# Two row tiles of TensorE: another order of seven products, another giver for one semaphore

## The chip, the cores and the metric

The kernel runs on one NeuronCore of a Trainium2 chip. The metric is the device time of one execution in microseconds (us), median of several runs. Engines are named as in the profile: PE is TensorE's matmul, PEld its weight load, DVE is VectorE, ACT is ScalarE, POOL is GpSimd, SP issues the DMAs.

## The reference

Sigmoid attention over 8 batches, 12 heads, 448 tokens and head width 64, and after it a gated feed-forward layer over the 3584 tokens (768 to 1536 to 768):

```python
scores = scale * np.matmul(q, k.transpose(0, 1, 3, 2)) - np.log(S)
attn = 1.0 / (1.0 + np.exp(-scores))
x = np.matmul(attn, v)                       # (8, 12, 448, 64) -> (3584, 768)
...
gate = 1.0 / (1.0 + np.exp(-(x @ w_gate)))
val = x @ w_val
y = gate * val @ w_out
```

All inputs are float32 (the three weights arrive as 64-bit words, which DVE turns into float32 on the chip).

## The kernel before

**Two stages.** Attention takes the first 257 us; in it, scores and values are matmuls of 64x64 tiles (lines 208 and 224). After a g-th block of scores, `LAG` = 2 blocks later, comes the same block of values. PSUM then holds two score buffers of two banks (`sc`) and four one-bank sums of values (tags `av00`, `av01`, `av10`, `av11`). The rest, the feed-forward layer, is the helper at line 341: 9072 matmuls of 64 rows by 128 columns by 448 tokens.

**Seven products.** Each matrix product of the layer is cut into 2x2 blocks and done with seven block products instead of eight (Strassen's scheme in Winograd's form). x and the weights come as seven sums of blocks each; product i multiplies the i-th of both. Products are summed in PSUM as far as they can be: 1 is added onto 0, 3 and 4 onto 2, 6 onto 5. So an accumulator begins at 0, 2 and 5 and is read after *every* product, since each partial sum is wanted: product 0 gives `s1`, 1 the block "11", 2 `u2`, 3 `u3`, 4 a new `s1`, 5 a new `u3`, 6 a new `u2`. A product that adds onto an accumulator may start only when the sum before it has been read out of the bank (evacuated) by DVE (line 391) or ACT (lines 515 and 522).

**Input stage** (to about 880 us): three passes `s` over the hidden blocks, in each four pairs of batches `p`, in each seven products `i`, in each four accumulators `q` (gate and value of two hidden blocks). A *unit* is one accumulator of one product: 3 blocks of 128 rows x 3 terms. The terms are there because float32 operands are split into a high and a low part in a faster format, and three of the four products of parts are summed. ACT makes the high part (line 169 for x, 417 for weights), DVE the low part (172, 420).

**Output stage** (from about 880 us): four pairs, seven products, in each two halves of the hidden blocks, in each three accumulators `o`. Half 1 adds onto half 0 without evacuation between.

**Two row tiles.** The 128 rows of TensorE are used as two tiles of 64 rows that work at the same time. Of every unit, nine matmuls go to the upper tile (lane 0: partitions 0 to 63 of weights and x) and nine to the lower tile (lane 1: partitions 64 to 127), onto the *same* accumulator. They must not meet in that bank, so the lower nine come later: `BEHIND` = 12 matmuls behind. `Lanes.push` writes the instruction stream: one upper matmul of the unit at hand, one lower matmul of an earlier unit, in turn. So the lower lane begins a unit just after the upper lane has issued the fourth matmul of the unit that follows.

**Semaphores between the lanes.** `mark` lets a matmul raise a lane's semaphore when it is done (the drain is fused into the matmul issued last), and notes for an accumulator which count means that its matmuls are done. `follow` waits for that count. Before, the mark of an upper half hangs on the *second matmul of the next* upper unit (`n == 1`, line 372), that of a lower half on the second matmul of the next lower unit (line 358). The first lower matmul of a unit waits for lane 0's mark, the first upper matmul of a product that adds onto an accumulator waits for lane 1's mark and for the engine that evacuated the bank.

**What sets the order of the rest.** DVE, ACT and POOL get their work unit by unit, in the order in which lower halves are finished: `after_in` (input stage) and `after_out` (output stage) issue the evacuation of the unit, then the preparation of the x operand two products ahead, now and then the low part of a weight tile (`low_w`), and steps of the weight conversion (lines 116 to 134) at an even rate. Each engine works its list in order. DMAs stand in SP's queue.

Of the kernel before, what the change touches and what calls it, by code (L numbers as in the profile page):

```python
# [17 lines left out]
P = 128  # L18
# [10 lines left out]

NP = 7  # L30


@with_exitstack
def sigmoid_attention_glu_kernel(ctx: ExitStack, tc: tile.TileContext, qk, v, wg, wv, wo, out):
# [123 lines left out]

    x_order = [(s, p, i) for s in range(NPASS) for p in range(NPAIR) for i in range(NP)]
    x_loaded, ops = {}, {}  # L160
# [24 lines left out]
    with tc.manual_schedule(), tc.tile_pool(name="att", bufs=2) as att, tc.tile_pool(name="sc", bufs=2, space=PSUM) as scp, \  # L185
# [9 lines left out]
        def load_v(m):  # L195
            if m < B * NQ:
                loads[m].append(att.tile([P, 7, 2, D], F32, tag="v", name="v"))
                if m > 0:
                    nc.sync.dma_start(out=loads[m][1], in_=v[m // NQ, m % NQ])

        def scores(m, g):
            qkt = loads[m][0]
            sc = scp.tile([P, 2, 512], F32, tag="sc", name="sc")
            for h in range(2):
                for u in range(2):
                    p = u if g == 3 else g // 4
                    k0 = S + (3 * P if g == 3 else g % 4 * P + u * HP)
                    nc.tensor.matmul(sc[halves[u], h, :S], lhsT=qkt[halves[h], p, k0:k0 + HP], rhs=qkt[halves[h], p, :S],  # L208
                                     start=True, stop=True)
            a = att.tile([P, 2, S], F32, tag="a", name="a", bufs=3)  # L210
            nc.scalar.activation(a, sc[:, :, :S], AF.Sigmoid, bias=bias, scale=scale)  # L211
            return a

        def values(m, g, a):
            vt = loads[m][1]
            for u in range(2):
                p = u if g == 3 else g // 4
                key = (2 * m + p, u)
                start = key not in avs
                if start:  # L220
                    avs[key] = avp.tile([P, 512], F32, tag=f"av{p}{u}", name="av")
                last = (3 if u == 0 else 2) if p == 0 else 6
                for h in range(2):
                    nc.tensor.matmul(avs[key][halves[h], :S], lhsT=vt[halves[u], g, h], rhs=a[halves[u], h],  # L224
                                     start=start, stop=g == last)
            if g == 3:
                finish(2 * m)
            if g == 6:
                finish(2 * m + 1)
# [85 lines left out]
    with tc.manual_schedule(), tc.tile_pool(name="mm", bufs=8, space=PSUM, reuse_waits="tile") as mm:  # L315
# [14 lines left out]
        class Lanes:  # L330


            def __init__(self):
                self.behind, self.skip, self.at, self.ended = [], BEHIND, 0, {}
                self.sems, self.count = [tc.alloc_semaphore(f"lane{h}") for h in range(2)], [0, 0]
                self.last = [None, None]

# [15 lines left out]
            def lower(self):  # L353
                unit, key, done = self.behind[0]
                if self.at == 0:
                    self.follow(key)
                ins = self.one(1, unit, self.at)
                if self.at == 1 and self.last[1] is not None:
                    self.mark(self.last[1], 1)
                self.at += 1  # L360
                if self.at == len(unit[1]):
                    self.last[1] = key
                    self.at = 0
# [3 lines left out]
            def push(self, unit, key, done):  # L367
                self.behind.append((unit, key, done))
                self.follow(key)
                for n in range(len(unit[1])):  # L370
                    ins = self.one(0, unit, n)
                    if n == 1 and self.last[0] is not None:
                        self.mark(self.last[0], 0)
                    if self.skip:
                        self.skip -= 1
                    else:
                        self.lower()
                self.last[0] = key

            def drain(self):  # L380
                self.mark(self.last[0], 0)
                while self.behind:
                    self.lower()
# [12 lines left out]
        nextW = {}  # L396
        o_order = [(p, i, h) for p in range(NPAIR) for i in range(NP) for h in range(2)]
        h_loaded, h_ops, wx = {}, {}, {}
# [28 lines left out]
        def fetch_wx(i):  # L427
            tag, bufs = (("wr", 3), ("wf", 2), ("wsum", 2))[0 if i < 3 else 1 if i < 5 else 2]
            wx[i] = block(tag, bufs, [P, HJ - NQUAD, 2, HW], F32R)
# [48 lines left out]
        def outputs():  # L478
            m = 0
            for p in range(NPAIR):  # L480
                st = [{} for _ in range(HC)]
                for i in range(NP):
                    if p == 0:
                        W[i] = nextW[i]
                    for half in range(2):
                        for o in range(HC):
                            d = st[o]
                            if half == 0 and i in (0, 2, 5):
                                d["acc"] = bank()
                            acc = d["acc"]  # L490
                            js = range(3 * half, 3 * half + 3)
# [5 lines left out]
        with tc.tile_pool(name="ff", bufs=1, reuse_waits="tile") as ff:  # L497
# [10 lines left out]
            def after_in(n, s, p, i, q, st, acc):  # L508
# [49 lines left out]
                if q == 3:  # L558
                    if p == NPAIR - 1:
# [3 lines left out]
                        else:  # L563
                            fetch_w(nextW[i], o_src[i][:, :NQUAD], (10, 10, 20, 22, 24, 26, 28)[i])
                    if 0 <= 2 * NP - 2 - left < NP:
                        fetch_wx(2 * NP - 2 - left)
                    if n + 1 < len(x_order):
                        ops.pop(n)
                if p < NPAIR - 1 and (s < NPASS - 1 or p < NPAIR - 2) and (s == 0 or p > 0 or i > 1):
                    groups += 1  # L570
# [4 lines left out]
            for n, (s, p, i) in enumerate(x_order):  # L575
                if i == 0:
                    st = [{} for _ in range(NQUAD)]
# [5 lines left out]
                for q in range(NQUAD):  # L583
                    if i in (0, 2, 5):
                        st[q]["acc"] = bank()
                    acc = st[q]["acc"]
                    lanes.push(terms(acc, [(W[i][:, q], ops[n], (cols(k), k)) for k in range(HC)], i), banks.index(acc),
# [52 lines left out]
```

## Time and profile before

| | |
|---|---|
| median of 3 runs | 1195.25 us (1194.55 to 1195.45) |
| the profiled execution's own time | 1196.26 us |
| its span, first to last instruction | 1194.4 us |
| PE, PEld busy | 1187.3 us (99%), 1017.1 us (85%) |
| DVE, ACT, POOL busy | 716.8 us (60%), 491.4 us (41%), 321.4 us (27%) |
| DMA | 266.82 MB, mean 223 GB/s |
| mean granted TensorE clock | 0.998 |

The times are those of one execution. A matmul's end is modelled and matmuls overlap, so "PE 99% busy" only says that some matmul was nearly always under way: how fast they follow each other is read from their count in a stretch of time. The timeline view merges instructions of one line that follow each other without a gap into one row: start, length, and how many (x). From such a row the pace follows as (length minus one matmul) / (count minus 1). The windows view counts the instructions that overlap a stretch, those under way at its start included.

### The profile page before, as it was taken

The page shows a single profiled execution, that of the slowest core. Times are in us where ns is not written, and L with a number is a line of the kernel's source. Part 1 is how long each engine was busy: PE and PEld are TensorE (multiplying, and loading weights), DVE is VectorE, ACT ScalarE, POOL GpSimd, SP SyncE. Part 2 cuts the span into 40 slices and gives each one's busy share as a digit, 9 for nine tenths or more (in the row PEclk, how much of TensorE's full clock was granted, in tenths as well). Part 3 has the DMA queues.
Part 4 walks back from the last instruction along what each step waited for, and adds up shares of the span by engine and source line. Part 5 has one row for each costly group of instructions (what it writes and reads, how often), then busy time and mean ns, then how long its engine had stood idle before and what let it go on. Part 6 is the DMA issues. An engine that isn't in the chain of part 4 may idle for free.

```text
span 1194.4 us, 27526 instructions
## 1 busy us (share of the span) xinstructions
PE 1187.3 (99%) x11776; PEld 1017.1 (85%) x11776; DVE 716.8 (60%) x827; ACT 491.4 (41%) x553; POOL 321.4 (27%) x244
## 2 busy tenths in 40 slices
PE   9999999999999999999999999999999999999998
PEld 3444444579999999999999999999999999999998
DVE  3344234426988858898885888846674533434343
ACT  6777777762323235232233523224435222142230
POOL 2162524251526144161632426133110000000000
PEclk9999999999999999999999999999999999999999
DMA  8585876876777687777858757566776444544531
GB/s 312 195 280 205 282 237 240 302 243 217 258 250 256 228 287 238 245 236 252 287 202 303 241 178 257 171 229 205 274 258 215 165 160 147 201 130 165 178 132 70
DMA packets 103257, 266.82 MB, mean 223 GB/s; under 512 B 10464, under 2 KB 74336, under 8 KB 103136
## 3 DMA queue, kind: packets, MB, share of 16 engines
q1 hardware_dynamic: 102992, 264.95, 65.2%
q8 instruction: 93, 1.52, 0.5%
q14 instruction: 28, 0.23, 0.1%
q10 hardware_dynamic: 144, 0.11, 0.0%
HBM read 176.95 MB, written 88.08 MB: 222 GB/s over the span
## 4 chain that ended last, share of the span: by engine, by line
PE 97%; DVE 2%; ACT 0%; issue 0%; DMA 0%; DVEq 0%
PE acc L341 76%; PE sc L208 11%; PE av L224 11%; DVE op L172 0%; DVE u L391 0%; DMA qk<-qk 0%; DVE w L420 0%; DVE wf L116 0%; DVE wf L117 0%; DVE wsum L420 0%; DVE s L391 0%; ACT w L417 0%; DVE s L394 0%; ACT op L169 0%; ACT a L211 0%
## 5 line engine op out<-in xcount | busy, mean ns | idle before, releaser
L341 PE MATMUL acc<-op,w 64*128 64x448 f32 x8064 | 913.0, 363 | 2.5 <-DVE u L391 2.4
L341 PEld LDWEIGHTS acc<-op,w 64*128 64x128 f32 x8064 | 863.2, 184 | 27.3 <-issue 3.6
L172 DVE TENSOR_TENSOR op<-src,op 128x1344 fp32r<-128x1344 f32 x140 | 231.3, 1663 | 78.8 <-ACT op L169 57.4
L169 ACT CAST op<-src 128x1344 fp32r<-128x1344 f32 x140 | 182.1, 1315 | 202.5 <-PE acc L341 180.4
L211 ACT ACTIVATE a<-sc,bias 128x896 f32<-128x896 f32 x168 | 169.2, 1008 | 64.3 <-PE sc L208 60.5
L208 PE MATMUL sc<-qk 64*64 64x448 f32 x1344 | 160.9, 540 | 0.2
L224 PE MATMUL av<-a,v 64*64 64x448 f32 x1344 | 159.7, 536 | 0.0
L391 DVE TENSOR_TENSOR u<-acc,s 128x448 f32<-128x448 f32 x120 | 74.5, 622 | 98.2 <-PE acc L341 97.7
L208 PEld LDWEIGHTS sc<-qk 64*64 64x64 f32 x1344 | 55.9, 134 | 72.0 <-issue 56.5
L224 PEld LDWEIGHTS av<-a,v 64*64 64x64 f32 x1344 | 56.5, 133 | 70.0 <-issue 65.8
L391 DVE TENSOR_TENSOR u<-acc,u 128x448 f32<-128x448 f32 (+1 forms) x121 | 73.8, 616 | 64.8 <-PE acc L341 64.6
L542 POOL TENSOR_TENSOR t<-u,v 128x448 f32<-128x448 f32 x23 | 34.6, 1505 | 234.1 <-DVE u L394 234.1
L341 PE MATMUL acc<-op,wr 64*128 64x448 f32 x432 | 81.3, 362 | 0.0
L134 POOL TENSOR_TENSOR wsum<-wf 128x384 f32<-128x384 f32 x18 | 21.0, 1169 | 219.3 <-DVE wf L122 219.3
L535 ACT ACTIVATE u<-u 128x448 f32<-128x448 f32 x48 | 27.8, 579 | 120.1 <-DVE u L391 118.8
L341 PEld LDWEIGHTS acc<-op,wr 64*128 64x128 f32 x432 | 69.2, 184 | 0.8
L535 ACT ACTIVATE s<-s 128x448 f32<-128x448 f32 x24 | 13.9, 579 | 119.6 <-DVE s L391 119.6
L391 DVE TENSOR_TENSOR s<-acc,s 128x448 f32<-128x448 f32 x60 | 37.2, 622 | 39.5 <-PE acc L341 39.2
L341 PE MATMUL acc<-op,wsum 64*128 64x448 f32 x288 | 54.0, 362 | 0.0
L341 PE MATMUL acc<-op,wf 64*128 64x448 f32 x288 | 53.8, 362 | 0.0
L250 DVE TENSOR_TENSOR op<-av,op 128x448 f32<-128x448 f32 x24 | 14.9, 622 | 54.0 <-ACT op L241 54.0
L341 PEld LDWEIGHTS acc<-op,wsum 64*128 64x128 f32 x288 | 46.1, 184 | 0.9
(51 smaller groups left out, 750.7 us busy)
## 6 DMA issues: line engine op xcount, KB each, us to landing
src<-xs SPq DMA_DIRECT2D x84, 672.0 KB, 4.7
src<-hs SPq DMA_DIRECT2D x56, 672.0 KB, 4.5
hs<-t SPq DMA_DIRECT2D x96, 224.0 KB, 5.4
qk<-qk SPq DMA_DIRECT2D x23, 896.0 KB, 5.1
xs<-t SPq DMA_DIRECT2D x48, 224.0 KB, 4.0
w<-ws SPq DMA_DIRECT2D x14, 768.0 KB, 7.1
v<-vv SPq DMA_DIRECT2D x23, 448.0 KB, 4.5
wr<-wg SPq DMA_DIRECT2D x12, 768.0 KB, 6.4
```

The lines of the kernel that those rows point to most:

```text
L134: nc.gpsimd.tensor_tensor(out=s1, in0=a21, in1=a22, op=ALU.add)
L169: nc.scalar.copy(op[:, 0], src)
L172: nc.vector.tensor_tensor(out=op[:, 1], in0=src, in1=op[:, 0].bitcast(F32), op=ALU.subtract)
L208: nc.tensor.matmul(sc[halves[u], h, :S], lhsT=qkt[halves[h], p, k0:k0 + HP], rhs=qkt[halves[h], p, :S], start=True, stop=True)
L211: nc.scalar.activation(a, sc[:, :, :S], AF.Sigmoid, bias=bias, scale=scale)
L224: nc.tensor.matmul(avs[key][halves[h], :S], lhsT=vt[halves[u], g, h], rhs=a[halves[u], h], start=start, stop=g == last)
L250: nc.vector.tensor_tensor(out=x, in0=other, in1=x, op=ALU.add)
L341: return nc.tensor.matmul(acc, lhsT=a[halves[h]], rhs=b[halves[h]], start=start and h == 0 and n == 0, stop=stop and h == 1 and n == len(p ...
L391: nc.vector.tensor_tensor(out=o, in0=a, in1=b, op=ALU.add)
L535: nc.scalar.activation(d[k], d[k], AF.Sigmoid)
L542: nc.gpsimd.tensor_tensor(out=o, in0=a, in1=b, op=ALU.subtract)
```

## The change

- The seven products are done in the order 0, 2, 1, 3, 5, 4, 6 instead of 0 to 6, in both stages; loads of x, hidden blocks and weights follow that order (the tables of delays and buffers are indexed by the place in it). Which product adds onto which accumulator is written out in `CHAIN`; it is the same as before.
- The mark of an upper half hangs on the last matmul of that half itself (`n == len - 1`). A lower half gets a mark only where an upper half waits for it without an evacuation between, that is between the two halves of the hidden blocks in the output stage; it hangs on the *first* matmul of the next lower unit.
- In attention, the two sums `av10` and `av11` become one tile of two banks, and the third block of scores of the whole kernel (`(m, g) == (0, LAG)`) uses that tile as a third score buffer.

```diff
+ORDER = (0, 2, 1, 3, 5, 4, 6)
+CHAIN = (0, 0, 2, 2, 2, 5, 5)
...
-    x_order = [(s, p, i) for s in range(NPASS) for p in range(NPAIR) for i in range(NP)]
+    x_order = [(s, p, i) for s in range(NPASS) for p in range(NPAIR) for i in ORDER]
...
+        def second_pair():
+            return avp.tile([P, 2, 512], F32, tag="av1", name="av")
...
-            sc = scp.tile([P, 2, 512], F32, tag="sc", name="sc")
+            sc = second_pair() if (m, g) == (0, LAG) else scp.tile([P, 2, 512], F32, tag="sc", name="sc")
...
-                start = key not in avs
-                if start:
-                    avs[key] = avp.tile([P, 512], F32, tag=f"av{p}{u}", name="av")
+                start = g == (3 + (u == 0) if p else 0)
+                if start and p == 0:
+                    avs[key] = avp.tile([P, 512], F32, tag=f"av0{u}", name="av")
+                elif start and u == 1:
+                    pair = second_pair()
+                    avs.update({(2 * m + p, w): pair[:, w] for w in range(2)})
...
             def lower(self):
...
-                ins = self.one(1, unit, self.at)
-                if self.at == 1 and self.last[1] is not None:
-                    self.mark(self.last[1], 1)
+                self.one(1, unit, self.at)
+                if self.at == 0 and self.open is not None:
+                    self.mark(self.open, 1)
+                    self.open = None
                 self.at += 1
                 if self.at == len(unit[1]):
-                    self.last[1] = key
+                    self.open = None if unit[3] else key
...
             def push(self, unit, key, done):
...
                 for n in range(len(unit[1])):
-                    ins = self.one(0, unit, n)
-                    if n == 1 and self.last[0] is not None:
-                        self.mark(self.last[0], 0)
+                    self.one(0, unit, n)
+                    if n == len(unit[1]) - 1:
+                        self.mark(key, 0)
...
-                for i in range(NP):
+                for i in ORDER:
...
-                                d["acc"] = bank()
-                            acc = d["acc"]
+                                d[i] = bank()
+                            acc = d[CHAIN[i]]
```

What the order of instructions shows of it, first on PE, in the input stage, at the first upper matmul of product 6 in the last pass and the last pair (weight tile w6; names are accumulators, x operands and weights with their buffer numbers; rows between are left out). Before:

```order
L341 MATMUL acc_11780<-op_11655,w5_8854 128x448 [waits Activation_49]
...
L341 MATMUL acc_11834<-op_11655,w5_8854 128x448
L341 MATMUL acc_11780<-op_11762,w6_8977 128x448 [waits DVE_49,lane1,Activation_49]
L341 MATMUL acc_11834<-op_11655,w5_8854 128x448
L341 MATMUL acc_11780<-op_11762,w6_8977 128x448
```

After the change:

```order
L352 MATMUL acc_11328<-op_11206,w5_8508 128x448 [waits Activation_49]
...
L352 MATMUL acc_11011<-op_11310,w4_8611 128x448 [waits DVE_49,lane0,Activation_49]
...
L352 MATMUL acc_11067<-op_11310,w4_8611 128x448
L352 MATMUL acc_11328<-op_11413,w6_8730 128x448 [waits DVE_49,lane0,Activation_49]
L352 MATMUL acc_11067<-op_11310,w4_8611 128x448
```

Before, product 6 adds onto the accumulator that product 5 began four units earlier. After, product 4 stands between, so the accumulator was begun eight units earlier; the wait for lane 1 has become one for lane 0's count.

The second place is DVE's list there, around the low parts of two weight tiles. Before:

```order
L394 TENSOR_TENSOR s1_11380<-s1_11380,s1_11352 128x448 [waits DVE_49,Activation_49]
L420 TENSOR_TENSOR w1_11495<-w1_11495 128x4x384 [waits DMAHW0_49]
L420 TENSOR_TENSOR wsum_11497<-wsum_11497 128x2x384 [waits DMAHW1_49]
L391 TENSOR_TENSOR u3_11627<-acc_11780,u3_11627 128x448 [waits PE_49]
L391 TENSOR_TENSOR u3_11651<-acc_11806,u3_11651 128x448 [waits PE_49]
```

After:

```order
L401 TENSOR_TENSOR u3_11282<-acc_11328,u3_11282 128x448 [waits DVE_49,PE_49]
...
L404 TENSOR_TENSOR u3_11359<-u3_11359,u3_11335 128x448 [waits DVE_49,Activation_49]
L430 TENSOR_TENSOR w2_11155<-w2_11155 128x4x384 [waits DMAHW7_49]
L430 TENSOR_TENSOR wsum_11157<-wsum_11157 128x2x384 [waits DMAHW0_49]
L401 TENSOR_TENSOR s1_10967<-acc_11011,s1_10967 128x448 [waits PE_49]
```

Before, the evacuation for which product 6 waits (acc_11780) stands behind both weight tiles. After, the one for which product 6 waits (acc_11328) stands ahead of them, and behind them stands that of product 4 (acc_11011), on which no later product adds.

More of the change, by code (lines that the diff above doesn't have):

```diff
@@ L335, in __init__ @@
                 self.sems, self.count = [tc.alloc_semaphore(f"lane{h}") for h in range(2)], [0, 0]
-                self.last = [None, None]
+                self.open = None
             def one(self, h, unit, n):
@@ L356, in lower @@
                     self.follow(key)
-                ins = self.one(1, unit, self.at)
-                if self.at == 1 and self.last[1] is not None:
-                    self.mark(self.last[1], 1)
+                self.one(1, unit, self.at)
+                if self.at == 0 and self.open is not None:
+                    self.mark(self.open, 1)
+                    self.open = None
                 self.at += 1
                 if self.at == len(unit[1]):
-                    self.last[1] = key
+                    self.open = None if unit[3] else key
                     self.at = 0
@@ L377, in push @@
                         self.lower()
-                self.last[0] = key
             def drain(self):
-                self.mark(self.last[0], 0)
                 while self.behind:
@@ L396, in sigmoid_attention_glu_kernel @@
         nextW = {}
-        o_order = [(p, i, h) for p in range(NPAIR) for i in range(NP) for h in range(2)]
+        o_order = [(p, i, h) for p in range(NPAIR) for i in ORDER for h in range(2)]
         h_loaded, h_ops, wx = {}, {}, {}
@@ L427, in fetch_wx @@
         def fetch_wx(i):
-            tag, bufs = (("wr", 3), ("wf", 2), ("wsum", 2))[0 if i < 3 else 1 if i < 5 else 2]
+            tag, bufs = (("wr", 3), ("wf", 2), ("wsum", 2))[0 if ORDER.index(i) < 3 else 1 if ORDER.index(i) < 5 else 2]
             wx[i] = block(tag, bufs, [P, HJ - NQUAD, 2, HW], F32R)
@@ L563, in after_in @@
                         else:
-                            fetch_w(nextW[i], o_src[i][:, :NQUAD], (10, 10, 20, 22, 24, 26, 28)[i])
+                            fetch_w(nextW[i], o_src[i][:, :NQUAD], (10, 10, 20, 22, 24, 26, 28)[ORDER.index(i)])
                     if 0 <= 2 * NP - 2 - left < NP:
-                        fetch_wx(2 * NP - 2 - left)
+                        fetch_wx(ORDER[2 * NP - 2 - left])
                     if n + 1 < len(x_order):
                         ops.pop(n)
-                if p < NPAIR - 1 and (s < NPASS - 1 or p < NPAIR - 2) and (s == 0 or p > 0 or i > 1):
+                if p < NPAIR - 1 and (s < NPASS - 1 or p < NPAIR - 2) and (s == 0 or p > 0 or ORDER.index(i) > 1):
                     groups += 1
@@ L575, in sigmoid_attention_glu_kernel @@
             for n, (s, p, i) in enumerate(x_order):
-                if i == 0:
+                if i == ORDER[0]:
                     st = [{} for _ in range(NQUAD)]
@@ L584, in sigmoid_attention_glu_kernel @@
                     if i in (0, 2, 5):
-                        st[q]["acc"] = bank()
-                    acc = st[q]["acc"]
+                        st[q][i] = bank()
+                    acc = st[q][CHAIN[i]]
                     lanes.push(terms(acc, [(W[i][:, q], ops[n], (cols(k), k)) for k in range(HC)], i), banks.index(acc),
```

## The prediction

> **What bounds the kernel now.** First the engines' shares on the page, then the chain that ended last, in order of time (start, length, what):
>
> ```profile
> PE 1187.3 (99%) x11776; PEld 1017.1 (85%) x11776; DVE 716.8 (60%) x827; ACT 491.4 (41%) x553; POOL 321.4 (27%) x244
> 302.23 307.90 PE acc L341 x3001
> 611.45 1.38 DVE wf L116
> 615.30 84.87 PE acc L341 x817
> 709.07 2.23 DVE op L172
> 715.73 140.42 PE acc L341 x1364
> 868.65 1.67 DVE w L420
> 870.32 0.87 DVE wsum L420
> 871.87 319.06 PE acc L341 x3077
> ```
>
> PE carries the chain; in the feed-forward layer it is broken at a few places by DVE. So two questions: how much time do those breaks take, and how fast do matmuls follow each other between them? The groups of line 341 by operand give the frame (durations min/median/max in ns, first and last start), and merged rows of PE's timeline the pace:
>
> ```profile
> L341 PE MATMUL acc<-op,w x8064: 355/362/575, 257.9 to 1189.3; 64*128 64x448 f32 x197
> L341 PE MATMUL acc<-op,wsum x288: 355/362/369, 942.2 to 1190.6; 64*128 64x448 f32 x144
> 258.40 1.78 PE L341 MATMUL acc<-op,w 64*128 64x448 f32 x8
> 265.69 24.66 PE L341 MATMUL acc<-op,w 64*128 64x448 f32 x240
> 329.72 100.62 PE L341 MATMUL acc<-op,w 64*128 64x448 f32 x983
> 429.63 100.62 PE L341 MATMUL acc<-op,w 64*128 64x448 f32 x983
> 1189.32 1.22 PEld L341 LDWEIGHTS acc<-op,wsum 64*128 64x128 f32 x6
> ```
>
> All 9072 matmuls (8064 and 1008 on the other operands) start within 257.9 to 1190.6: 932.7 us for 4536 pairs, one upper and one lower. A pair takes 2 x (100.62 - 0.36) / 982 = 204.2 ns in the long steady stretches of the input stage, 2 x 24.30 / 239 = 203.3 ns shortly after its start. The upper lane alone, before the lower has begun, takes 1.42 / 7 = 203 ns a matmul, so two lanes cost no more than one; the lower lane alone, at the end, takes (1.22 - 0.18) / 5 = 208 ns, about 207 within the rounding. One lane thus knows a fast and a slow pace. The windows view (length, PE's busy time and count, clock, DMA share, GB/s) gives the output stage, the last two rows, and the stretches around the breaks:
>
> ```profile
> 299.00:305.00 6.00, 5.93 (x58) 1.00 0.78 265
> 612.00:619.00 7.00, 6.71 (x63) 1.00 0.32 108
> 695.00:702.00 7.00, 6.99 (x69) 1.00 0.28 99
> 711.00:718.00 7.00, 6.51 (x63) 1.00 0.62 218
> 867.00:877.00 10.00, 8.36 (x66) 0.83 0.74 238
> 873.00:874.00 1.00, 1.00 (x8) 0.50 1.06 401
> 912.00:920.00 8.00, 8.00 (x78) 1.00 0.10 31
> 926.00:931.00 5.00, 5.00 (x50) 1.00 0.02 3
> 1050.00:1100.00 50.00, 50.00 (x498) 1.00 0.50 166
> 1100.00:1150.00 50.00, 50.00 (x498) 1.00 0.45 153
> ```
>
> A count holds some 3.6 matmuls (363 / 102 ns) that were under way at the start. So the output stage has 494.4 in 50 us: 202.3 ns a pair, the fastest pace of the trace. At 102.1 ns a matmul the seven stretches (the one of 1 us at 873 apart) should show 62.4, 72.2, 72.2, 72.2, 101.6, 82 and 52.6; they lack 4.4, 9.2, 3.2, 9.2, 35.6, 4 and 2.6, together 68 matmuls or **6.9 us** of stalls. Half of it is at 870 us, where the clock falls too: 0.50 in the stretch from 873.
>
> **Why PE stalls**, at that place (DVE and PE rows of the timeline):
>
> ```profile
> 868.57 1.75 DVE L420 TENSOR_TENSOR w<-w 128x1536 fp32r<-128x1536 f32 x1
> 870.24 0.95 DVE L420 TENSOR_TENSOR wsum<-wsum 128x768 fp32r<-128x768 f32 x1
> 871.11 1.15 DVE L391 TENSOR_TENSOR u<-acc,u 128x448 f32<-128x448 f32 x2
> 871.87 1.61 PE L341 MATMUL acc<-op,w 64*128 64x448 f32 x10 [1.64 <-DVE u L391]
> ```
>
> The evacuation for which product 6 waits stands on DVE behind two low parts of weights, and PE resumes as soon as it is done. How late may an evacuation be? A unit is 9 pairs, 1.84 us. The next product's upper half on the same bank comes 4 units after this one's, 7.35 us. The lower half ends 12 + 9 pairs after the upper began, 4.3 us, plus the offset of the lanes (up to 0.2) and 0.36 for the last matmul: 4.85. So 2.5 us are left for a DVE operation of 0.62 with all that is queued ahead of it. In the output stage a bank's second half is followed by the next product after 3 units, 5.5 us: 0.7 are left, which explains the small stalls at 915 and 928.
>
> **The change, part by part.**
>
> *Order of the products.* In 0 2 1 3 5 4 6 every addition onto a bank comes two products after the one before it (0 to 1, 2 to 3, 3 to 4, 5 to 6), and each set of banks is taken anew two products after its last use. So 8 units instead of 4: 14.7 us, 9.85 left for the evacuation; 9 units instead of 3 in the output stage, 11.6 left. The worst evacuation above was late by its 2.5 us of slack and PE's 2 of stall, 4.5 us, under half of the new slack. DVE, ACT, POOL and the DMAs do the same operations, none added. One buffer is asked for earlier: `u2` comes one product (7.35 us) sooner, and its buffer may still be read by POOL's sums of the seven products before. In the pass with the least room:
>
> ```profile
> 522.20 1.48 POOL L542 TENSOR_TENSOR t<-u,u 128x448 f32<-128x448 f32 x1
> 538.55 0.63 DVE L391 TENSOR_TENSOR u<-acc,s 128x448 f32<-128x448 f32 x1 [0.43 <-PE acc L341]
> ```
>
> POOL has read it at 523.7, DVE would write it at 538.55 - 7.35 = 531.2: 7.5 us of room, no new wait. So the stalls go: **-6.9 us**, bounds 0 and -6.9. I take the full value, since the same lists with 7 us more of slack leave none of the seven; the drop of the clock goes with them.
>
> *The mark of an upper half.* Before, the first lower matmul of a unit waits for a matmul that starts only two pairs (0.41 us) ahead of it and takes 0.36; its weight load should begin about one pair earlier still. So this wait is always late, 504 times, and behind it in TensorE's one instruction stream stand the weight loads of both lanes. It seldom costs a lane much, since a lane's weights are loaded while its matmul before runs (0.2 us), but it shifts the lanes against each other, and I read the mixture of paces, 202.3, 203.3 and 204.2 with equal instructions, as what comes of it. After, the mark is two matmuls earlier, given 0.81 - 0.36 = 0.45 us ahead of the matmul that needs it. That covers a weight load:
>
> ```profile
> L341 PEld LDWEIGHTS acc<-op,w x8064: 182/184/331, 257.9 to 1189.1; 64*128 64x128 f32 x197
> L341 PEldq EVENT_SEMAPHORE  x49: 51/51/51, 256.9 to 1176.9; - x49
> ```
>
> With the wait out of the way each lane keeps its own pace. The mean pace now is (932.7 - 6.9 - 2.4) / 4536 = 203.6 ns; the 2.4 are the 24 matmuls in which one lane runs alone at either end, 24 x 0.101, which stay. Bounds for the new pace: 202.3, the output stage (-5.9 us), and 207, the lone lower lane (+15.4). I take 202.7, next to the lone upper lane (203 within its rounding) that starts as freshly as both lanes will, and to the output stage: **-4.1 us**.
>
> *Fewer marks and waits.* Lane 1's marks fall from 503 to 84 (3 accumulators x 7 products x 4 pairs); 240 upper halves now wait for a lane 0 count that is products old, so for nothing. The separate semaphore instructions (49 x 51 ns, 2.5 us if all were on the path) run ahead in PE's queue, under the matmuls: 0, bounds -2.5 and +2.5. The Trainium skill ("TensorE: Matmul & The Clock Gate", "The cost: per-tile semaphore tail") says that increments on concurrent tiles follow one another at 26.3 ns each; by it, 419 fewer would give an estimated 11.0 us more, and the sum would be 1173 instead of 1184. This trace speaks against such a price on the path: the output stage has both marks in every unit and the fastest pace, 202.3.
>
> *Third score buffer*, at the kernel's start:
>
> ```profile
> 3.59 3.88 PE L208 MATMUL sc<-qk 64*64 64x448 f32 x24
> 6.49 0.21 PEld L208 LDWEIGHTS sc<-qk 64*64 64x64 f32 x8 [1.10 <-ACT a L211]
> ```
>
> At 6.49 the third block's weight loads waited 1.10 us for ACT to free a buffer, but PE's matmuls run on without a gap from 3.59. Bounds 0 and -1.1; nearest is the row without a gap, I take **-0.2**. Later in attention the pair of banks is asked for four blocks (6 us) after its last read, as before: 0.
>
> *Sum:* 6.9 + 4.1 + 0.2 = 11.2. From the profiled execution's 1196.26 that makes 1185.1; the median of the runs is 1.0 under that execution, so **1184.1 us**.
>
> **The rivals.**
>
> *The stalls go, the pace stays.* If the lanes' mixture of paces isn't the late wait's doing but their own (operand addresses, say), 203.6 stays and only 7.1 us are won: 1188.1. For it: equal waits in the output stage go with 202.3. Against it: equal matmuls in one stage run at 203.3 and 204.2. Chance 0.2.
>
> *The lanes settle on the slow pace: slower.* Nothing nudges a lane any more after its start, so one that falls into 207 stays there, as the lower lane does at the end, and the queue's order holds the other to it. All through, 4536 x 3.4 ns = +15.4, less 7.1: 1203.5. It loses from a mean pace of 203.6 + 7100 / 4536 = 205.2 on. Against it: where lanes start afresh, at 258.40, they start fast. Chance 0.12.
>
> *The stalls only move.* The order gives no slack where it was needed: DVE's list at those places is late by more than 10 us, or another operation at the same place (a weight's low part, a load) is what PE then waits for. Then at most 2 us are won, 1193.5. Against it: each break of the chain ends in an evacuation. Chance 0.1.
>
> *Marks cost time of their own*, up to the whole gain in pace and more, by the mechanism weighed above: each of 419 marks not given would have to save 17 ns, the 1.9 ns between 204.2 and 202.3 over nine pairs, 7.1 us: 1181.0. Chance 0.03.
>
> **How the numbers follow.** The forecast gets the other 0.55. The range of 8 in 10 goes from 1181.5 (best pace and a little more) to 1191.5, which takes in the first rival and stalls that go only in half; outside are the slow pace, most of the moved stalls, and the marks' price. Within 0.2%, 2.4 us, is about what can't be told from no change. Faster: forecast, first and last rival and a fifth of the third, 0.8; the same: the rest of the third, 0.08; slower: 0.12.
>
> **What would show it.** The chain should run through the feed-forward layer in one piece, with no DVE between; the counts around the product boundaries should not dip, and the clock stay at 1.00 around 870 us. Rows like 329.72 with x983 should hold 989 or more matmuls in the same time (202.7); at 204.2 the first rival is right, near 970 the second. Wrong would be breaks with DVE at other places, or PE waiting for a DMA or for ACT.

## The result and the profile after the change

The changed kernel takes **1202.8 us** (median of four runs, 1202.1 to 1204.11), the kernel before 1195.35 beside it (four runs, 1194.55 to 1197.32): a ratio of 1.0061, with a 95% interval of 1.0044 to 1.0079. It is slower by 0.6%. The forecast was 1184.1; the rival "the lanes settle on the slow pace" had 1203.5. The profiled execution took 1204.11, with a span of 1202.3. Three executions that took far longer than all others are left out of the medians in this text: one of the kernel before (1693.53 us), a first one of "one late mark in 28 units" (3242.27, its matmuls 750 ns long) and one of the old order with 10 behind (4241.75).

First, the page of the changed kernel: engines' shares, and the group of line 352, where the feed-forward matmuls now are (busy time, mean ns, idle time before). Then the one row of the feed-forward layer in its chain of waits:

```profile
PE 1196.5 (100%) x11776; PEld 1083.8 (90%) x11776; DVE 718.7 (60%) x827; ACT 489.4 (41%) x553; POOL 314.9 (26%) x244
...
L352 PE MATMUL acc<-op,w 64*128 64x448 f32 x8064 | 894.8, 366 | 0.0
```

```profile
259.02 939.80 PE acc L352 x9072
```

The breaks by DVE are gone: the layer is one piece of 9072 matmuls. But the piece is 939.8 us long; before, the same matmuls took 932.7 from first to last start with all their stalls. The windows of the prediction, now of the changed kernel (length, PE's busy time and count, clock, DMA share, GB/s):

```profile
612.00:619.00 7.00, 7.00 (x71) 1.00 0.81 272
867.00:877.00 10.00, 10.00 (x101) 1.00 0.51 162
873.00:874.00 1.00, 1.00 (x13) 1.00 0.00 0
...
300.00:400.00 100.00, 100.00 (x971) 1.00 0.75 252
400.00:500.00 100.00, 100.00 (x971) 1.00 0.73 249
1050.00:1100.00 50.00, 50.00 (x487) 1.00 0.42 140
1100.00:1150.00 50.00, 50.00 (x487) 1.00 0.49 164
```

Around 870 us no dip is left, 101 where it was 66, and the clock stays at 1.00. Everywhere else the counts are *lower* than before: 971 - 3.6 matmuls in 100 us make 206.7 ns a pair, and 487 - 3.6 in 50 us 206.9, where the output stage had 498 (202.3). It is one pace for 940 us. The pace is there before the lower lane has begun; PE's timeline of the changed kernel, in a stretch with the upper lane alone:

```profile
259.66 1.60 PE L352 MATMUL acc<-op,w 64*128 64x448 f32 x7
```

(1.60 - 0.36) / 6 = 206.7 ns a matmul (0.36 is one matmul, as in the prediction), where the kernel before started with 203.

So the difference of the two profiled executions, 1204.11 - 1196.26 = 7.85 us, is 6.84 in the feed-forward layer (939.50 from first to last start, against 932.66) and 1.0 in attention. The first is a loss and a gain. By the prediction's own reckoning (2.5 us off for the 24 matmuls in which a lane is alone) the pair now takes 937.0 / 4536 = 206.57 ns; over 203.55 before, that is +13.7 us, and the stalls that went are -6.9, together +6.8. The second is a break at 80 us that belongs to this execution and not to the change; it is taken up with the third score buffer below.

Single instructions of the changed kernel show which lane sets the pace. The lanes are told apart by the semaphores that some instructions carry, and between these by their steps; a lane's *step* is the time from the start of one of its matmuls to the start of the next. Starts in us, most weight loads left out:

```
803.813  upper matmul, the last of its unit: gives lane 0's mark
803.900  lower matmul
804.020  upper matmul
804.103  lower matmul
804.226  upper matmul
804.229  weight load, upper
804.234  weight load, lower: waited for lane 0's mark
804.300  lower matmul
804.433  upper matmul
804.540  lower matmul
```

The upper lane steps by 206 to 207 ns, across the wait too: nothing holds it up. The lower lane steps by 202 to 203 ns, runs ahead, and at the first load of each unit stands until the mark has come, 421 ns after the marking matmul's start. Over a unit its steps are 251, 202, 203, 199, 206, 203, 202, 203, 197, or 240 in front; nine of them make 1.86 us, the upper lane's nine. The slow lane is the upper one, which never waits; the fast one is held by the wait.

### The profile page after: what moved, and what is told of

Same layout as the page of the kernel before. It is cut to its first block, busy times and chain, and to the rows that moved or that the text cites. A ratio compares the mean times of both kernels' runs of the same rounds, so it can differ in the third digit from the quotient of the medians.

```text
span 1202.3 us, 27417 instructions
## 1 busy us (share of the span) xinstructions
PE 1196.5 (100%) x11776; PEld 1083.8 (90%) x11776; DVE 718.7 (60%) x827; ACT 489.4 (41%) x553; POOL 314.9 (26%) x244
## 4 chain that ended last, share of the span: by engine, by line
PE 98%; POOL 1%; DVE 0%; issue 0%; DMA 0%; ACT 0%; DVEq 0%; ACTq 0%
PE acc L352 78%; PE av L235 10%; PE sc L216 10%; POOL t L266 1%; DVE w L147 0%; DMA qk<-qk 0%; POOL wsum L137 0%; ACT a L219 0%; POOL wsum L138 0%; PE av L216 0%; DVE x L261 0%; DVE op L261 0%; POOL w L146 0%; ACT x L252 0%; DVE u L401 0%
## 5 line engine op out<-in xcount | busy, mean ns | idle before, releaser
L352 PE MATMUL acc<-op,w 64*128 64x448 f32 x8064 | 894.8, 366 | 0.0
L235 PE MATMUL av<-a,v 64*64 64x448 f32 x1344 | 224.5, 536 | 1.1 <-DVE op L261 1.1
L216 PE MATMUL sc<-qk 64*64 64x448 f32 x1336 | 223.4, 538 | 0.2 <-DMA qk<-qk 0.2
L216 PEld LDWEIGHTS sc<-qk 64*64 64x64 f32 x1336 | 82.7, 133 | 56.2 <-issue 29.8
L235 PEld LDWEIGHTS av<-a,v 64*64 64x64 f32 x1344 | 84.4, 133 | 43.4 <-issue 26.1
L352 PE MATMUL acc<-op,wr 64*128 64x448 f32 x432 | 73.5, 363 | 0.0
L352 PEld LDWEIGHTS acc<-op,wr 64*128 64x128 f32 x432 | 61.7, 184 | 0.0
L532 ACT ACTIVATE g<-acc 128x448 f32<-128x448 f32 x24 | 13.1, 546 | 105.2 <-PE acc L352 105.2
L352 PE MATMUL acc<-op,wsum 64*128 64x448 f32 x288 | 49.0, 363 | 0.0
L525 ACT COPY s<-acc 128x448 f32<-128x448 f32 x48 | 25.6, 533 | 53.0 <-PE acc L352 51.0
```

Source lines behind the costliest of these rows:

```text
L352: return nc.tensor.matmul(acc, lhsT=a[halves[h]], rhs=b[halves[h]], start=start and h == 0 and n == 0, stop=stop and h == 1 and n == len(p ...
L525: nc.scalar.copy(d["s1"], acc)
```

## The experiments

Three theories stood at the start. *A*: a lane has two paces, 202.7 and 206.67 ns, and holds the one it is in until something holds it up; the mark of the kernel before came so late (two pairs ahead of the matmul that waits) that every unit held up both lanes, which kept taking them out of the slow pace. *B*: the slow pace comes with the new order of products and its operands. *C*: it comes with the marks that lane 1 no longer gives. Each run's own time for the kernel before stands in its ratio.

**The order of products alone** (marks and attention of the kernel before).

```diff
 (the kernel before, with)
+ORDER = (0, 2, 1, 3, 5, 4, 6)
+CHAIN = (0, 0, 2, 2, 2, 5, 5)
 (...)
```

> The kernel before with the new order of the products alone; marks, waits and the attention stage as before. Theory A (the late mark of before, one per unit, breaks up the slow pace of 206.67 ns a pair, and the changed mark no longer does): no stalls at product boundaries and a mean pace of 202.3 to 204.2 ns, so 1184 to 1190 us. Rival B (the slow pace comes with the new order, from operands that now meet): 206.67 ns in every stretch, 1202 to 1204 us.

1191.97 us (ten runs, 1183.19 to 1194.18), ratio 0.9942 (0.9916 to 0.9968). The runs fall in two groups: four at 1183.2 to 1183.5, six at 1191.9 to 1194.2. The profiled execution is of the second (1192.45). Its windows, and its row in the chain of waits:

```profile
867.00:877.00 10.00, 10.00 (x102) 1.00 0.83 281
...
300.00:400.00 100.00, 100.00 (x983) 1.00 0.78 260
400.00:500.00 100.00, 100.00 (x982) 1.00 0.74 249
```

```profile
258.33 928.83 PE acc L345 x9062
```

The stalls are gone by the order alone. The pace is 204.2 (400 / (982 + 983 - 7.2) = 0.2043 us), never 206.7: rival B falls. By the starts of single matmuls it was 202.2 from 260 to 283 us, with a lower matmul some 150 to 200 ns behind its partner (the upper matmul written just ahead of it), and 204.2 from there on, with 240 to 300. At 204.2 a layer without stalls should take 4536 x 0.2042 + 2.4 = 928.7 us, and it took 928.53. That the group at 1183 is runs that kept the first pace is not shown: no profile of one was kept.

**The marks alone** (products 0 to 6, attention of the kernel before).

```diff
 (the kernel before, with)
-                    if n == 1 and self.last[0] is not None:
-                        self.mark(self.last[0], 0)
+                    if n == len(unit[1]) - 1:
+                        self.mark(key, 0)
 (and lane 1's marks of the change)
```

> The kernel before with the new marks alone, products in the order 0 to 6. Theory A: 206.67 ns a pair in all stretches between stalls, the stalls of before still there (each may throw a lane into the fast pace for a while), 1200 to 1211 us. Rival B (the slow pace comes with the order of the products): paces and stalls of before, 1194 to 1196 us.

1198.07 us (ten runs, 1191.05 to 1201.59), ratio 1.0009 (0.9989 to 1.0029): the edit that was to bring 4.1 us brings none in the mean, and the runs are spread over 10 us. What they are spread over stands in the windows of the profiled execution (1198.42):

```profile
400.00:600.00 200.00, 200.00 (x1939) 1.00 0.76 250
...
630.00:690.00 60.00, 60.00 (x596) 1.00 0.79 274
740.00:850.00 110.00, 110.00 (x1069) 1.00 0.63 210
```

```profile
612.00:619.00 7.00, 6.79 (x66) 1.00 0.62 228
...
711.00:718.00 7.00, 6.70 (x67) 1.00 0.59 207
867.00:877.00 10.00, 8.53 (x81) 1.00 0.62 196
...
940.00:1140.00 200.00, 200.00 (x1976) 1.00 0.49 165
```

206.7 ns for 200 us and more, then 202.6 for 60, then 206.5 for 110, and in the output stage 202.8 (by the starts of single matmuls 202.67 from 940 us to the end). Between these stretches stand the stalls at the product boundaries, which this kernel still has (66, 67 and 81 matmuls where 72, 72 and 102 would be). There are two paces with equal instructions, each held for a hundred us and more, and a stall can change one into the other.

**The lower lane 10 matmuls behind** (the changed kernel, but the mark is again two pairs ahead of the matmul that waits for it).

```diff
-BEHIND = 12
+BEHIND = 10
```

> The changed kernel with the lower lane 10 matmuls behind the upper instead of 12. Order, marks and their number are those of the change, but a lower half's first matmul now comes two pairs after the mark it waits for, as before the change, instead of four. Theory A: its wait is late again, the pace falls to 202.3 to 204.2 ns and the stalls stay away, 1184 to 1190 us. Rival C (the pace is lost by giving lane 1 fewer marks, whatever their place): 206.67 ns, 1202 to 1204 us. Rival B expects the same as C.

1182.28 us (four runs, 1182.08 to 1183.0), ratio **0.9891** (0.9875 to 0.9908). Lane 1's few marks and the new order are both in it, so B and C fall. Its chain and its windows:

```profile
257.29 919.71 PE acc L352 x9072
```

```profile
300.00:400.00 100.00, 100.00 (x993) 1.00 0.79 264
800.00:900.00 100.00, 100.00 (x993) 1.00 0.76 259
1050.00:1150.00 100.00, 100.00 (x993) 1.00 0.49 165
```

One piece, 20.1 us shorter than with 12 behind, at 200 / 989.4 = 202.1 ns a pair (202.2 by the starts). In this trace both lanes repeat the same nine steps in every unit (upper 203, 204, 197, 203, 202, 199, 207, 203, 202; lower 196, 199, 207, 203, 202, 203, 199, 206, 205), with the lower matmul always 133 to 142 ns behind its upper partner: each unit's late mark puts both back in the same place.

**One late mark in 28 units.**

```diff
 (...)
+                    if n == 1 and self.late is not None:
+                        self.mark(self.late, 0)
+                        self.late = None
                     if n == len(unit[1]) - 1:
-                        self.mark(key, 0)
+                        self.units += 1
+                        if self.units % 28 == 20:
+                            self.late = key
+                        else:
+                            self.mark(key, 0)
```

> The changed kernel with one edit: of every 28th unit the mark of its upper half is given late, by the second matmul of the upper half after it, as in the kernel before; the 27 units between have the changed mark. Theory A (a lane holds one of two paces, about 202.7 and 206.67 ns a pair, and goes from one to the other only where both lanes are held up together, which a late mark does): the trace shows stretches of 27 units (about 50 us) of constant pace, and the pace changes, if at all, at the late marks, so both paces are found; with half the stretches fast the time is about 1194, between 1186 (all fast) and 1203 (none). The rival (the pace comes with something else that the kernel before had at every unit, or with an operand): 206.67 ns everywhere and 1202 to 1204 us, as without the 18 late marks.

1193.26 us (one run). Late marks fall near 294, 345, 397, 448, 500 us, and so on. The windows between them:

```profile
302.00:342.00 40.00, 40.00 (x398) 1.00 0.88 293
378.00:395.00 17.00, 17.00 (x168) 1.00 0.65 232
396.00:399.00 3.00, 3.00 (x31) 1.00 1.00 372
402.00:442.00 40.00, 40.00 (x398) 1.00 0.80 269
446.00:462.00 16.00, 16.00 (x161) 1.00 0.67 227
480.00:497.00 17.00, 17.00 (x168) 1.00 0.64 216
505.00:545.00 40.00, 40.00 (x398) 1.00 0.74 256
```

Fast and slow take turns: 394.4 matmuls in 40 us (202.8 ns), then 164.4 in 17 (206.8), and again. In single instructions the turn is this. After the late mark at 294 both lanes step by 202.7, and keep it. The one at 345 puts the lower lane to 206.7; the upper stays at 202.7, so the lower falls back by 4 ns a pair, from 278 ns behind its partner to some 700 at 371 us, and from then on holds the upper one to its own pace. The one at 397 comes when the lanes stand so far apart that it holds up the upper lane too (two steps of 521 and 306 ns); both go on at 202.7. So it goes on to the end, and no lane changes its pace by itself between two late marks. That is theory A, and its 1194 for half the stretches fast (one run alone, but its own trace shows the turns).

**11 behind, 9 behind**: the mark three pairs ahead of the matmul that waits, and one.

```diff
-BEHIND = 12
+BEHIND = 11      (in the other kernel: 9)
```

> The changed kernel with the lower lane 11 matmuls behind the upper one instead of 12, so that the mark is given three pairs ahead of the lower matmul that waits for it (four in the changed kernel; two with 10, where 1182.3 us and 202.3 ns a pair were measured). Theory A (the upper lane is corrected only where a lower weight load waits so long that the upper lane's own next load, queued behind it, is late too): a load that waits goes on about 420 ns after the marking matmul's start, and the upper load behind it is due about 610 ns after it, so the upper lane is not held up; the pace is one that holds itself, 206.67 ns (about 1203 us) or 202.7 (about 1185), constant over hundreds of us, not the 202.3 of 10 behind. The rival (a later mark is better by degrees, whatever is held up): between 202.3 and 206.67 ns at every stretch, about 1192 us.

> The changed kernel with the lower lane 9 behind: the lower matmul that waits is written just one pair behind the matmul that gives the mark. A waiting weight load goes on about 420 ns after the start of the marking matmul; the upper lane's next but one load, queued behind it, is due about 250 ns after it, so the wait now holds up both lanes for well over 100 ns in each of 504 units: theory A says 124 ns a unit, 13.8 a pair, 216 ns a pair and 1245 us. The rival (a late mark corrects the lanes without a price, whatever its lateness): 202.2 ns, 1182 us.

With 11 behind: 1202.2 us (four runs, 1201.39 to 1202.64), ratio 1.005 (1.0035 to 1.0065). With 9 behind: 1246.16 us (one run). The windows of 11 behind, and then of 9 behind:

```profile
262.00:292.00 30.00, 30.00 (x299) 1.00 0.75 246
340.00:440.00 100.00, 100.00 (x972) 1.00 0.73 245
700.00:800.00 100.00, 100.00 (x972) 1.00 0.64 211
```

```profile
300.00:400.00 100.00, 100.00 (x928) 1.00 0.72 241
400.00:500.00 100.00, 100.00 (x928) 1.00 0.72 237
```

With three pairs the lanes start at 203 and less; at 299 us the lower one changes to 206.7 with no stall near it, falls back until the upper one must follow, and there both stay to the end, 206.7 ns. With one pair the wait holds up both lanes in each unit: 216.3 ns a pair, 127 ns a unit more than at 202.2, 983.1 us for the layer; expected were 124 and 1245 us. So the time over the mark's lead is no slope: 1246 at one pair, 1182 at two, 1202 at three, 1203 at four. The rivals, by which a later mark is better by degrees or costs nothing (1192 with 11, 1182 with 9), miss at both ends.

**10 behind with the old order of products** (and without the third score buffer).

```diff
 (the kernel with the marks alone, with)
-BEHIND = 12
+BEHIND = 10
```

> The kernel before (products 0 to 6, its attention) with the changed marks and the lower lane 10 behind. It tells how much of the gain of 10 behind is pace and how much the order of the products. Theory A: the mark again comes two pairs ahead of the matmul that waits for it, so the pace is 202.2 to 202.4 ns a pair between the product boundaries, and the stalls at these stay, about 6 us (a little less than 6.9, since the lower half ends 0.4 us earlier): 1188 to 1190 us. The rival (the order of operands is needed for the fast pace): 203.5 to 204.2 ns between the boundaries, 1194 to 1197 us.

1192.24 us (median of five runs, 1189.2 to 1194.41), ratio 0.9961 (0.9943 to 0.9979). Both expectations are half right. Its start shows a correction at work; PE's timeline, with the upper lane alone:

```profile
258.07 1.81 PE L341 MATMUL acc<-op,w 64*128 64x448 f32 x8
```

(1.81 - 0.36) / 7 = 207 ns: the lane begins at the slow pace, as in the changed kernel. Single steps are 206 or 207 until the lower lane begins at 259.93 us, then two of 210, and from 260.6 on nine of them make 1.82 us, 202.2 each. In the changed kernel, with the mark four pairs ahead, a lane that started so stayed at 206.7 for 940 us. The windows:

```profile
264.00:296.00 32.00, 32.00 (x320) 1.00 0.71 248
350.00:450.00 100.00, 100.00 (x982) 1.00 0.77 258
620.00:690.00 70.00, 70.00 (x695) 1.00 0.80 274
740.00:840.00 100.00, 100.00 (x983) 1.00 0.62 202
```

```profile
605.00:620.00 15.00, 15.00 (x145) 1.00 0.58 202
695.00:715.00 20.00, 19.83 (x195) 1.00 0.49 175
862.00:877.00 15.00, 13.75 (x134) 1.00 0.65 212
```

At the start (316.4 in 32 us) and from 620 (691.4 in 70 us) the pace is 202.3 to 202.5, otherwise 204.2 to 204.4. It changes at 301 us, where the upper lane has steps of 245 and 280 ns at a product boundary, and again at the stalls near 614 and 713. So a late mark does not give one pace but at least two: 202.2 with the lower lane 140 ns behind its partner, and 204.2 with 240 to 300 ns, the pace that the kernel before had most of the time. A late evacuation can throw the lanes from the first into the second; with the order alone they came there at 283 us without one. The order of products is thus worth more than its stalls: 10.5 us lie between the layer of this profile (929.9) and that of 10 behind (919.4). At 102.1 ns a matmul the last three windows lack 5.5, 4.5 and 16.5 matmuls, 2.7 us of stalls, less than half of the 6.9 of the kernel before; the other 7.8 are pace.

**All marks late with the new order; 10 behind with lane 1's marks.** The first tells the two groups of the order alone from those of 10 behind, the second is its counterpart.

```diff
 (the changed kernel, every upper half marked late)
-                    if n == len(unit[1]) - 1:
-                        self.mark(key, 0)
+                    if n == 1 and self.late is not None:
+                        self.mark(self.late, 0)
 (...)
+                self.late = key
 (the other kernel: 10 behind, with)
-                if self.at == 0 and self.open is not None:
+                if self.at == 1 and self.open is not None:
                     self.mark(self.open, 1)
-                    self.open = None
-                    self.open = None if unit[3] else key
+                    self.open = key
```

> The changed kernel with one edit: every upper half is marked by the second matmul of the next upper half, as in the kernel before; lane 1 has the few marks of the change. It differs from the kernel with the new order alone (1191.97 us, in some runs 1183, in others 1192 to 1194) by lane 1's marks and by the third score buffer. Theory D (with a late mark the lanes have two regimes: offset held at about 140 ns and 202.2 ns a pair, or offset 240 to 300 and 204.2, and what throws them out of the first is the traffic of lane 1's marks): 202.2 all through, 1182 to 1183, as with 10 behind. Rival E (lane 1's marks are not it; 12 behind instead of 10 leaves the offset to drift): both regimes again, in one run 1183, in another 1192.

> The changed kernel with the lower lane 10 behind and with lane 1's marks as in the kernel before (each lower half, by the second matmul of the next). The counterpart of the run with all marks late. Theory D (lane 1's marks throw the lanes out of the regime of 202.2 ns): 204.2 ns in some or all executions, 1190 to 1192 us in these. Rival E (they do not): 202.2 ns and 1182 to 1183 us in every execution. A price of 17 ns for each of 419 marks on the path, which the prediction's last rival would need, would give 202.2 + 1.9 = 204.1 ns too, but then at a constant offset of the lanes and in every execution.

All marks late: 1191.17 us (six runs, five at 1190.04 to 1191.67 and one at 1183.75), ratio 0.9943 (0.9921 to 0.9964). 10 behind with lane 1's marks: 1182.72 (four runs, 1182.05 to 1183.24), ratio 0.988 (0.9863 to 0.9896), 202.2 ns. Theory D falls, rival E stands: lane 1's marks are not what loses the fast regime (202.2 ns, the lower lane some 140 ns behind its partner). They cost nothing either, 419 more and no time. The times of the first fall in two groups again, as E says, but its profiled execution (1190.04) is in neither of the two regimes named:

```profile
300.00:400.00 100.00, 100.00 (x985) 1.00 0.78 263
```

That is 203.8 ns, 203.7 by the starts and the same to the end, with the lower lane 129 to 199 ns behind its partner. So two regimes are too few.

**10 behind without the third score buffer, and 10 behind once more.**

```diff
 (10 behind, with attention as in the kernel before)
 (...)
-            sc = second_pair() if (m, g) == (0, LAG) else scp.tile([P, 2, 512], F32, tag="sc", name="sc")
+            sc = scp.tile([P, 2, 512], F32, tag="sc", name="sc")
```

> The changed kernel with the lower lane 10 behind, but without the third score buffer (attention's sums and score buffers as in the kernel before). It measures what the third buffer is worth. As predicted at 0.2 us, with bounds 0 and 1.1: 1182.5, between 1182.3 and 1183.4 us, with the feed-forward layer as in 10 behind (202.2 to 202.3 ns a pair). The rival (the buffer starts PE's work without a break, so that the clock is granted earlier, which saved about 1 us in the first 20 us of the changed kernel): 1183.3 or more.

> The changed kernel with the lower lane 10 behind once more, for how far its 1182.28 us hold: theory A (the regime of 202.2 ns holds itself where no evacuation is late, so it is lost in no execution): 1182 to 1183 us in all. The rival (it is one of two regimes and was met by chance): some executions at 1190 to 1192, as with the new order alone.

Without the buffer: 1184.32 us (four runs, 1182.55 to 1188.32), ratio 0.9906 (0.9882 to 0.9929). With it, once more: 1183.37 (four runs, 1182.53 to 1185.07), ratio 0.9889 (0.9873 to 0.9905). The intervals overlap, and the buffer's worth is not told from nothing by times. Both profiled executions have 919.4 us for the feed-forward layer, to 0.01 us, and both have the same break in attention. It is in the changed kernel's profiled execution too; its chain of waits there, the row of its waits, and, from 10 behind without the break (1182.28), DVE's row for the same operation:

```profile
78.49 3.08 DVE w L147
81.57 0.55 DVE op L261
...
82.16 0.59 PE av L235 x2
```

```profile
PE av L235 <- DVE op L261: 1.1, 1, 1.1
```

```profile
78.83 0.83 DVE L147 TENSOR_TENSOR w<-wf,w 128x384 fp32r<-128x384 f32 x1 [7.98 <-POOL w L146]
```

DVE starts its low part of a weight block (line 147) at 78.5 to 79.6 us, as in the others (78.6 to 79.9), but takes 3.08 or 3.09 us for it where they take 0.82 or 0.83; PE's values wait for the DVE operation behind it, with 1.67 us between two matmuls. POOL works on the same blocks (line 146) at that time in all of them, and why DVE is held up in some is open. Three of thirteen profiled executions have the break, one of them without the third buffer; the rest, old and new, have not. It does not go with an edit, and the 1.0 us that attention lost above is this break less a gain at the start. Without the break, attention takes, from its first matmul to the layer's first, 253.8 to 254.5 us with two score buffers (four executions) and 253.2 to 254.5 with three (six): the means are 254.2 and 253.8.

## Why the prediction was wrong

**The order of products** was right. The stalls were to go in full, -6.9 us; the changed kernel has none, and the kernel with the order alone has none at the pace of 204.2. Its reason held too, the same lists with 7 us more of slack. What the step did not see is that a stall also sets the pace of what follows it.

**The mark of an upper half** is the step that failed: forecast -4.1 us, measured +13.7 (206.57 ns a pair instead of the 202.7 assumed). Three parts of it are to be told apart.

- "I read the mixture of paces [...] as what comes of" the late wait: right. Marks two pairs ahead gave 202.2, 203.7 or 204.2, marks three or four pairs ahead 202.7 or 206.7.
- "With the wait out of the way each lane keeps its own pace": right, and that is the loss. A lane nearly always keeps whichever pace it has, and the late wait that the change removed was what took the lanes out of the slow one. The prediction priced it as a disturbance; by the traces it was a correction that cost little: with 10 behind it is there 504 times at 202.2 ns. What corrects is a late wait in every unit: of the single late marks in 28 units every other one put the lower lane into the slow pace.
- "I take 202.7, next to the lone upper lane [...] that starts as freshly as both lanes will": wrong. A lane that starts afresh is not always fast. The lone upper lane took 206.7 at its start in this kernel and in that with 10 behind and the old order, and 203 in the kernel before and in that with 11 behind. Nor does a fast start last: with 11 behind it lasted 40 us, and once a lane had slipped, nothing in the next 880 us brought it back. A row of 1.78 us was taken for the state of 940.

The wait was not out of the way either. The prediction found the mark 0.45 us ahead, enough to cover a weight load. That holds for a lane that keeps its place behind the other; the lower lane runs up to the wait and is held there, by 40 to 50 ns in each unit. It is harmless, for that lane has the time to lose.

**The rival "the lanes settle on the slow pace"** came true, 1203.5 forecast and 1202.8 measured, with the pace that it named (207) and the point from which it loses (205.2). What it had otherwise is who holds whom: it named a slow lower lane, as at the end of the kernel before, and the queue's order that holds the other to it; here the upper is slow, and the wait for its mark holds the lower. With 11 behind the lower is slow. What the prediction set against it, that lanes start fast where they start afresh, is the sentence that failed above. What spoke for it stood in the same rows: the lone lower lane at about 207, and no row of a lane that went from 207 to 203 without a stall or a late mark.

**"The stalls go, the pace stays"** had 1188.1, and the order without the marks took 1191.97; but that median stands for two groups, at 1183 and 1192, and no run lies at 1188. **"The stalls only move"** is refuted by a chain without a break.

**Marks.** Forecast 0, measured 0: with 10 behind, 419 more marks make 1182.72 against 1183.37 beside it. The Trainium skill ("TensorE: Matmul & The Clock Gate", "The cost: per-tile semaphore tail") has 26.3 ns for each increment, by which these runs would lie an estimated 11.0 us apart; on the path that ends this kernel no run shows it. **The third score buffer**: forecast -0.2, between the means of the executions without the break -0.4, within their spread.

Left open: why a late mark with 12 behind loses the fast regime in most executions and with 10 behind in none of twelve (two times four runs, and four with lane 1's marks; of four without the third buffer one took 1188.32), though the mark leads the wait by two pairs in both; why the paces under late marks are 202.2, 203.7 or 204.2; and what in the hardware makes a lane's step 202.7 or 206.7 ns. That the wait for the mark stands at the head of the upper lane's loads is inferred from the stream of instructions and borne out by 9, 10 and 11 behind; no row shows a blocked load by itself.

**What is best.** The changed kernel with the lower lane 10 behind takes 1182.28 us (0.9891 of the kernel before, 0.9875 to 0.9908), and 1183.37 when run once more: 1.1% under the kernel before and 1.7% under the changed one. Two things make it: the order of products takes away what disturbs the lanes, and the mark two pairs ahead, a lead that the kernel before had too, puts them back in step in each unit.

## What to carry to other kernels

A wait that is always a little late can be what keeps two streams in step: before it is moved away, find out which of the two states each stream falls into when it is left alone, over the whole run and not over its first microseconds. Where a trace shows several paces with equal instructions, treat them as states and look for what changes one into the other; the price of an edit is then the share of time in each state, not a mean. Trying a few leads of the mark (here one, two, three, four pairs: 1246, 1182, 1202, 1203 us) costs a number in one line and tells more than the argument did.

## What the hardware showed unexpectedly

- Two row tiles at the same work do not keep the order in which their matmuls are written. The lower matmul that stands behind an upper one in the stream starts 340 ns *before* it in the changed kernel, 140 ns after it with 10 behind, and up to 700 ns after it in the slow stretches between late marks.
- A lane's matmul of 448 columns with a new 64x128 weight tile has two steps, 202.7 and 206.67 ns on average, at a granted clock of 1.00 in both. Each was seen to last for hundreds of us (202.7 from 940 us to the end with the marks alone, 206.67 for 940 us in the changed kernel); fast became slow by itself (299 us, 11 behind), slow became fast only at a stall or a late mark, and a late mark could make fast slow too (345 us, one late mark in 28 units).
- A weight load that waits for a semaphore of the other lane starts 417 to 421 ns after the start of the marking matmul (about 365 ns long), with 9, 10 and 12 behind.
- With a correction in each unit (10 behind) the pair takes 202.2 ns, less than either lane left alone, 202.7.
